# The last loads in another order, and one block of w2 loaded in mid-stream as 125 rows and 3 rows

## The chip, the core and the metric

The kernel runs on one core of one Trainium2 chip. The metric is the device time of one execution in microseconds (us), as the median of several runs. The engines of the core work side by side: TensorE (PE: matrix products, its weight loads are PEld), VectorE (DVE), ScalarE (ACT), GpSimd (POOL) and SyncE (SP), whose queue issues all the transfers of this kernel. The transfers themselves are carried by 16 DMA engines, from HBM (the large memory) into SBUF (the on-chip memory of 128 partitions). PSUM is where TensorE leaves its sums. Everything is 32-bit floating point.

## The reference, cut to what matters

One decode step of a transformer block with a modulated layer norm: one token, D = 640, 32 heads of 192, a cache of 8192 positions, a feed-forward width F = 1536.

```python
mod = (silu(c) @ w_mod).reshape(1, 6, 1, -1)        # w_mod: 640 x 3840
sa, ca, ga, sb, cb, gb = mod[:, 0], ..., mod[:, 5]
h = layernorm(x) * (1 + ca) + sa
# attention: q = h @ wq; scores against k_cache, softmax, sum over v_cache, then @ wo
x = x + ga * attention(h, k_cache, v_cache, wq, wo)
h = layernorm(x) * (1 + cb) + sb
r = relu(h @ w1 + b1)                               # w1: 640 x 1536
x = x + gb * ((r * r) @ w2 + b2)                    # w2: 1536 x 640
```

The keys and the values are 32 x 8192 x 192 numbers each, 403 MB together; with all weights the kernel reads 452 MB once.

## The kernel before, in words

**The stream.** The host packs everything into few arrays whose rows belong to the 128 partitions. `plan()` cuts keys, values and the blocks of wq and wo that belong to them into 53 chunks of at most 84 x 192 numbers per partition (`SLOT`); a chunk is a tuple (first key, keys, first value unit, value units, extra blocks). `load(n)` (line 210 issues) takes the next of three buffers (`slot`, three in rotation) and issues the transfer on SP's queue; the last chunk goes in two pieces. After the 53 chunks three more loads follow, each into the next of the same three buffers, and each cut in pieces at the columns of a tuple:

- `wm1_t`: the last pair's block of wo (1920 columns) and the modulation columns 2 to 4, in two pieces (`WM_CUT`): 3840 KB and 1920 KB;
- `w1_t`: the modulation column 5 (for gb, 3200 columns) and w1 (5 blocks of 1536 columns), in two pieces (`W1_CUT`): 3904 KB and 1536 KB;
- `w2_t`: w2 as 12 blocks of 640 columns, in three pieces (`W2_CUT`): 2560, 960 and 320 KB, the last of them a single block.

`load(n + 3)` stands at the end of the turn of chunk n, so a load is issued when the work on the chunk three before it, which used the same buffer, is done. So wm1 goes into the buffer of chunk 50, w1 into that of 51 and w2 into that of 52.

**A chunk's work.** DVE multiplies keys by the query (line 249; the query stands in the ring `qb`) and sums (257), with a part of the sum begun on POOL (376). `softmax` follows when a head is complete; `values` adds the value units on PE (298), `evict` and `turn` bring a head pair's result into columns, and `attend` (331, 333) multiplies it by the pair's block of wo into the PSUM tile `att_a`.

**The end, in program order.** After the last chunk: `evict`, `turn(15)` and `attend(15)` with the block of wo in `wm1_t`; `mod(2, 3, ...)` (line 179), five steps of four matmuls for modulation columns 2 to 4, with `gather()` before its fourth step, which brings `att_a` through `att_s` into the layout of the rest (340 to 346); x1 (414, 415); `layernorm` "ln2": two sums over the partitions by a matmul with ones (line 137), with DVE work before, between and after; `columns`, which is DVE's transpose into hT (122). Then `gate(5, gb_t)` (188, 192): ten matmuls for gb and four copies by ACT. Then `ps_f` (428), 20 matmuls with w1; bias, relu and square on DVE (431 to 433), transpose (122); one matmul `ps_warm` whose result nobody reads (438); `ps_y` (446), 48 matmuls with w2, block b = 0 to 11 in order; two DVE steps (449, 450) and the output transfer (451).

The order of the work on each engine is the program order (`manual_schedule`); waits between engines are set by what each instruction reads and writes.

Of the kernel before, what the change touches and what calls it, by code (L numbers as in the profile page):

```python
# [8 lines left out]
F32 = mybir.dt.float32  # L9
# [4 lines left out]
P = 128  # L14
D = 640
H = 32
SK = 8192
DH = 192
FF = 1536
G = 4  # L20
DG = D // G
FG = FF // G
KB = DG // 32
FB = FG // 32
# [4 lines left out]
NPAIR = H // 2  # L29
NPOS = SK // P  # L30
POOL = 7
WO = 3 * D
QC = 512
NQ = H * DH // QC
RING = 3 * QC
SRING = 4 * NPOS
WQ = KB * QC
UNIT = E * DH
SLOT = 84 * DH
VPC = 5  # L40
LEAD_FROM = 1300
LEAD = 120
W1_CUT = (KB * D + 3 * FF, KB * D + KB * FF)
W2_CUT = (8 * D, 11 * D, 12 * D)
WM_CUT = (WO + 9 * D, WO + 15 * D)
WARM = 1
EPS = 1e-5


def plan():  # L50

    chunks, kp, vp, q, o = [], 0, 0, 1, 0
    while kp < H * NPOS or vp < H * NPOS // E:
        room, w = SLOT, []
        if o < NPAIR - 1 and 2 * (o + 1) * NPOS // E <= vp:
            w.append(("o", o))
            o, room = o + 1, room - WO
        used = (QC * (q - 2) - 1) // DH + 1 if q > 2 else 0
        if q < NQ and kp >= NPOS * (QC * q // DH) - 3 * NPOS // 2 and kp >= NPOS * used:
            w.append(("q", q))  # L60
            q, room = q + 1, room - WQ
        if not chunks:
            nk, nv = NPOS, 0
        else:
            v = VPC - 1 if kp >= LEAD_FROM else VPC
            nk = min(H * NPOS - kp, (room - v * UNIT) // DH)
            if kp + nk - E * (vp + v) > LEAD:
                v += 1
                nk = min(H * NPOS - kp, (room - v * UNIT) // DH)
            nv = min(H * NPOS // E - vp, (room - nk * DH) // UNIT)  # L70
            while nv and ((vp + nv - 1) // (NPOS // E) + 1) * NPOS > kp + nk:
                nv -= 1
            nk = min(H * NPOS - kp, (room - nv * UNIT) // DH)
        chunks.append((kp, nk, vp, nv, w))
        kp, vp = kp + nk, vp + nv
    assert q == NQ and o == NPAIR - 1
    return chunks


def width(chunk):  # L80
    return chunk[1] * DH + chunk[3] * UNIT + sum(WO if t == "o" else WQ for t, _ in chunk[4])


PLAN = plan()


@with_exitstack
def block_kernel(ctx: ExitStack, tc: tile.TileContext, kv, wm0, wm1, w1, w2, out):
    nc = tc.nc
    const = ctx.enter_context(tc.tile_pool(name="const", bufs=1))  # L90
    strm = ctx.enter_context(tc.tile_pool(name="strm", bufs=3))
    work = ctx.enter_context(tc.tile_pool(name="work", bufs=2))
    psum = ctx.enter_context(tc.tile_pool(name="psum", bufs=1, space=bass.MemoryType.PSUM))
# [25 lines left out]
    def columns(src, n, name, pool=const, **how):  # L119

        t = pool.tile([P, n // 32, 32], F32, name=name, **how)
        nc.vector.transpose(t.rearrange("p b r -> p (b r)"), src)
        return t
# [9 lines left out]
    def total(src, name):  # L133

        n = src.shape[1]
        ps = psum.tile([P, 512], F32, tag="sm", name="ps_" + name, bufs=2)
        nc.tensor.matmul(ps[:, :n], ones, src, start=True, stop=True)
        return ps[:, :n]

    def layernorm(x, copies, scale1, shift, name):  # L140

        n = x.shape[1]
        s = const.tile([P, 1], F32, name=name + "_s")
        nc.vector.tensor_reduce(s, x, axis=AX.X, op=ALU.add)
        m = const.tile([P, 1], F32, name=name + "_m")
        tm = total(s, name + "_tm")
        nc.vector.tensor_scalar(m, tm, 1.0 / (copies * D), None, op0=ALU.mult)
        xm = const.tile([P, n], F32, name=name + "_xm")
        nc.vector.tensor_scalar(xm, x, m, None, op0=ALU.subtract)
        sq = const.tile([P, n], F32, name=name + "_sq")  # L150
        ss = const.tile([P, 1], F32, name=name + "_ss")
        nc.vector.scalar_tensor_tensor(sq, xm, 1.0, xm, op0=ALU.mult, op1=ALU.mult, accum_out=ss)
        sd = const.tile([P, 1], F32, name=name + "_sd")
        nc.scalar.activation(sd, total(ss, name + "_tv"), AF.Sqrt, bias=eps_t, scale=1.0 / (copies * D))
        rs = const.tile([P, 1], F32, name=name + "_rs")
        nc.vector.reciprocal(rs, sd)
        h = const.tile([P, n], F32, name=name + "_h")
        nc.vector.scalar_tensor_tensor(h, xm, rs, scale1(), op0=ALU.mult, op1=ALU.mult)
        nc.vector.tensor_add(h, h, shift())
        return h  # L160
# [19 lines left out]
                                 wb[:, :, DG * g:DG * (g + 1)], start=(b == 0), stop=(b == KB - 1))  # L180
        nc.vector.tensor_copy(mods[:, first:first + n], ps[:, :n * DG].rearrange("p (m n) -> p m n", m=n))

    def gate(m, w):

        ps = psum.tile([P, 512], F32, tag="q", name=f"ps_mod{m}", bufs=2)
        for b in range(KB):
            for k in range(2):
                nc.tensor.matmul(ps[64 * k:64 * (k + 1), :2 * DG], e[:, b:b + 1].to_broadcast([P, 64]),  # L188
                                 w[:, b, 2 * DG * k:2 * DG * (k + 1)], start=(b == 0), stop=(b == KB - 1))
        for g in range(G):  # L190
            r = slice(32 * g, 32 * (g + 1))
            nc.scalar.activation(mods[r, m], ps[r, DG * (g % 2):DG * (g % 2 + 1)], AF.Copy)

    chunk_t = {}
    start = [sum(width(c) for c in PLAN[:n]) * P for n in range(len(PLAN))]

    def load(n):
        if n < len(PLAN):
            chunk_t[n] = slot(f"chunk{n}")
            m = width(PLAN[n])  # L200
            cuts = (m,) if n + 1 < len(PLAN) else ((PLAN[n][3] + 1) // 2 * UNIT, m)
            pieces = [(kv[start[n]:start[n] + P * m].rearrange("(p n) -> p n", p=P), cuts)]
        else:
            name, src, cuts = (("wm1_t", wm1, WM_CUT), ("w1_t", w1, W1_CUT), ("w2_t", w2, W2_CUT))[n - len(PLAN)]
            chunk_t[name] = slot(name)
            n, pieces = name, [(src, cuts)]
        for src, cuts in pieces:
            a = 0
            for b in cuts:
                nc.sync.dma_start(chunk_t[n][:, a:b], src[:, a:b])  # L210
                a = b
# [9 lines left out]
        return ca1  # L221

    h1 = layernorm(x_c, 1, scale_a, lambda: ma[:, :KB, 0], "ln1")
    qb = const.tile([P, RING], F32, name="qb")

    def query(u, w):
        w = w.rearrange("p (b n) -> p b n", b=KB)
# [4 lines left out]


    att_a = psum.tile([P, 512], F32, tag="att", name="att_a")
    att_s = const.tile([P, D], F32, name="att_s")
    nc.vector.memset(att_s, 0.0)
    query(0, wm0_t[:, KB * 2 * D:KB * 2 * D + WQ])

    sc = const.tile([P, SRING], F32, name="sc")
# [97 lines left out]

    def gather():

        nc.vector.tensor_copy(att_s[96:, :512], att_a[96:, :512])  # L340
        for j in range(NV):
            r = slice(32 * j, 32 * (j + 1))
            nc.scalar.activation(att_s[r, 512:], att_a[r, (D - 512) * j:(D - 512) * (j + 1)], AF.Copy)
        att_t.append(psum.tile([P, 512], F32, tag="o", name="att", bufs=3))
        for g in range(G):
            nc.tensor.matmul(att_t[0][32 * g:32 * (g + 1), :DG], sel.to_broadcast([P, 32]),
                             att_s[:, DG * g:DG * (g + 1)], start=True, stop=True)
# [6 lines left out]
    for n, (kp, nk, vp, nv, extra) in enumerate(PLAN):  # L354
# [3 lines left out]
        at = nk * DH + nv * UNIT  # L358
        wo_t = None
        for what, k in extra:  # L360
            w = t[:, at:at + (WO if what == "o" else WQ)]
            at += w.shape[1]
            if what == "q":
                query(k, w)
            else:
                wo_t = (k, w)
# [29 lines left out]
        for v in range(vp, vp + nv):  # L396
            if v % (NPOS // E) == NPOS // E - 1:
                to_evict.append(v // (NPOS // E))
        if wo_t is not None:
            attend(*wo_t)  # L400
        load(n + 3)

    wm1_t, w1_t, w2_t = chunk_t["wm1_t"], chunk_t["w1_t"], chunk_t["w2_t"]
    gb_t = w1_t[:, :KB * D].rearrange("p (b n) -> p b n", b=KB)
    w1_t = w1_t[:, KB * D:KB * (FF + D)].rearrange("p (b n) -> p b n", b=KB)
    w2_t = w2_t[:, :FB * D].rearrange("p (b n) -> p b n", b=FB)

    for h in to_evict:
        evict(h)
    turn(NPAIR - 1)  # L410
    attend(NPAIR - 1, wm1_t[:, :WO])
    mod(2, 3, wm1_t[:, WO:WO + KB * 3 * D].rearrange("p (b n) -> p b n", b=KB), gather)
    x1 = const.tile([P, DG], F32, name="x1")
    nc.vector.tensor_mul(x1, att_t[0][:, :DG], mods[:, 2])
    nc.vector.tensor_add(x1, x1, x_t)
# [3 lines left out]
        nc.vector.tensor_scalar(cb1, mods[:, 4], 1.0, None, op0=ALU.add)  # L419
        return cb1  # L420

    hT2 = columns(layernorm(x1, 32, scale_b, lambda: mods[:, 3], "ln2"), DG, "hT2")

    gate(5, gb_t)
    pf = psum.tile([P, 512], F32, tag="q", name="ps_f", bufs=2)
    for b in range(KB):
        for g in range(G):
# [5 lines left out]
    nc.vector.tensor_mul(f, f, f)  # L433
    fT = columns(f, FG, "fT", work, tag="om", bufs=1)

    idle = psum.tile([P, 512], F32, tag="sm", name="ps_warm", bufs=2)
    for k in range(WARM):
        nc.tensor.matmul(idle, ones, w1_t[:, k, :512], start=True, stop=True)
    gb2 = const.tile([P, DG], F32, name="gb2")
    nc.vector.tensor_mul(gb2, mods[:, 5], bbt[:, FG:])  # L440
    nc.vector.tensor_add(x1, x1, gb2)
# [1 line left out]
    py = psum.tile([P, 512], F32, tag="q", name="ps_y", bufs=2)  # L443
    for b in range(FB):
        for g in range(G):
            nc.tensor.matmul(py[32 * g:32 * (g + 1), :DG], fT[:, b], w2_t[:, b, DG * g:DG * (g + 1)],
                             start=(b == 0), stop=(b == FB - 1))
    y = const.tile([P, DG], F32, name="y")
    nc.vector.tensor_mul(y, py[:, :DG], mods[:, 5])
# [44 lines left out]
```

## Time and profile before

| | |
|---|---|
| median of 3 runs | 1056.03 us (1055.54 to 1056.21) |
| the profiled execution, its own time | 1055.57 us |
| its span, first to last instruction | 1053.8 us |
| busy: DVE, PE, POOL, ACT | 79%, 47%, 18%, 4% |
| DMA over the span | 452.15 MB, mean 429 GB/s |
| mean granted TensorE clock | 0.713 |

How to read it: the page cuts the span into 40 slices and gives in tenths how busy each engine was; the row of DMA engines stands at 9 in every slice but the last, where it is 7. The chain of work that ended last goes back from the last instruction, at each step to what released it. A view of the stretches gives, for chosen windows, each engine's busy time with its number of instructions, the granted clock, the mean busy share of the 16 DMA engines and their rate. The list of DMA issues gives the size of a transfer and the time from its issue on SP's queue to its landing. An instruction on PE that is written in 32-bit floating point shows as two records.

### The profile page before, as it was taken

Reading aid. Unit: us, or ns where it says so; the run is one execution under the profiler, and the core shown is the slowest. Engines: PE = TensorE matmul, PEld = TensorE weight load, DVE = VectorE, ACT = ScalarE, POOL = GpSimd, SP = SyncE. Lnnn points to the kernel's source line nnn. Section 1 sums busy time; section 2 is a strip of 40 time slices with the busy share of each in tenths; the row PEclk is TensorE's granted clock in tenths of the full one; section 3 lists DMA queues with packets and bytes.
Section 4 is the critical chain, followed back from the end, with each engine's and each line's share of the span. In section 5 each row is a group of like instructions: output and inputs, shape, how many; then the busy total and the mean of one; then the engine's idle time right before and its main releaser. Section 6 shows DMA issues by size and latency. Waiting matters only on the chain.

```text
span 1053.8 us, 5121 instructions
## 1 busy us (share of the span) xinstructions
PE 495.8 (47%) x2102; PEld 134.6 (13%) x2102; DVE 830.2 (79%) x428; ACT 43.4 (4%) x122; POOL 188.1 (18%) x57
## 2 busy tenths in 40 slices
PE   2153335455352363536344357344446346345286
PEld 1010011011010010101011011011011011011023
DVE  2898878877959969887797895999887977988822
ACT  1000000000000000000000000000000000000001
POOL 0212121121212202212121121122211211211200
PEclk9676576777675686668676577676777767768699
DMA  9999999999999999999999999999999999999997
GB/s 408 434 429 431 429 441 438 441 431 433 430 431 431 432 433 430 433 435 438 435 427 436 433 427 430 436 439 433 431 432 431 432 436 433 437 433 430 419 431 311
DMA packets 8959, 452.15 MB, mean 429 GB/s; under 512 B 996, under 2 KB 1000, under 8 KB 1256
## 3 DMA queue, kind: packets, MB, share of 16 engines
q1 hardware_dynamic: 8936, 451.83, 99.3%
q8 instruction: 16, 0.26, 0.1%
q14 instruction: 7, 0.06, 0.0%
HBM read 451.82 MB, written 0.00 MB: 429 GB/s over the span
## 4 chain that ended last, share of the span: by engine, by line
DMA 56%; DVE 31%; PE 11%; ACT 1%; issue 0%; SPq 0%; DVEq 0%
DMA chunk<-in_kv 53%; DVE chunk L249 16%; DVE sc L257 13%; PE ps_o L298 5%; DMA w_t<-in_w 2%; PE ps_q L230 2%; PE att_a L331 2%; DMA wm_t<-in_wm 1%; DVE os L312 1%; DVE om L310 1%; ACT p L281 0%; PE ps_mod L179 0%; PE ps_mx L273 0%; PE ps_mod L188 0%; PE att_a L333 0%
## 5 line engine op out<-in xcount | busy, mean ns | idle before, releaser
L249 DVE TENSOR_TENSOR chunk<-chunk,qb 128x8064 f32<-128x8064 f32 (+19 forms) x81 | 419.7, 5211 | 128.4 <-DMA chunk<-in_kv 123.2
L257 DVE TENSOR_REDUCE sc<-chunk 128x25 f32<-128x4800 f32 (+21 forms) x109 | 333.9, 3097 | 0.4
L298 PE MATMUL ps_o<-chunk,p 128*32 128x512 f32 x1536 | 296.7, 736 | 73.7 <-DMA chunk<-in_kv 64.3
L376 POOL TENSOR_TENSOR chunk<-chunk 128x1824 f32<-128x1824 f32 (+9 forms) x51 | 187.4, 3674 | 806.3 <-DVE chunk L249 548.4
L273 PE MATMUL ps_mx<-ident,mp 128*128 128x128 f32 x32 | 14.6, 455 | 343.9 <-DVE mp L271 343.9
L298 PEld LDWEIGHTS ps_o<-chunk,p 128*32 128x32 f32 x1536 | 67.4, 131 | 278.1 <-issue 188.1
L331 PE MATMUL att_a<-chunk,oT 128*32 128x512 f32 x90 | 63.4, 863 | 42.2 <-DVE oT L321 42.2
L230 PE MATMUL ps_q<-chunk,ln_h 128*128 128x512 f32 x110 | 66.9, 769 | 26.1 <-DMA chunk<-in_kv 26.1
L273 PEld LDWEIGHTS ps_mx<-ident,mp 128*128 128x128 f32 x32 | 5.6, 176 | 373.0 <-DVE mp L271 304.0
L281 ACT ACTIVATE p<-sc,nm 128x256 f32<-128x256 f32 x32 | 16.2, 507 | 649.9 <-DVE nm L275 649.9
L230 PEld LDWEIGHTS ps_q<-chunk,ln_h 128*128 128x128 f32 x110 | 26.5, 252 | 64.5 <-issue 35.1
L310 DVE TENSOR_TENSOR om<-ps_o,mask 96x512 f32<-96x512 f32 x32 | 21.6, 675 | 8.5 <-PE ps_o L298 8.5
L275 DVE TENSOR_REDUCE nm<-ps_mx 128x1 f32<-128x128 f32 x32 | 9.3, 292 | 19.5 <-PE ps_mx L273 19.5
L312 DVE TENSOR_REDUCE os<-om 96x64 f32<-96x512 f32 x32 | 21.8, 682 | 1.1
L331 PEld LDWEIGHTS att_a<-chunk,oT 128*32 128x32 f32 x90 | 11.7, 145 | 77.4 <-DVE oT L321 44.4
L320 DVE TENSOR_REDUCE oT<-ps_oT 128x3 f32<-128x96 f32 x16 | 4.0, 248 | 20.3 <-PE ps_oT L316 20.3
L286 PE MATMUL ps_sum<-ident,wide 128*128 128x128 f32 x16 | 7.5, 467 | 22.4 <-ACT wide L284 22.4
L179 PE MATMUL ps_mod<-wm_t,silu 128*32 128x320 f32 (+1 forms) x80 | 9.2, 608 | 15.5 <-DVE silu L167 15.5
L316 PE MATMUL ps_oT<-ident,os 96*128 96x96 f32 x16 | 5.0, 313 | 22.3 <-DVE os L312 22.3
L333 PE MATMUL att_a<-chunk,oW 128*96 128x384 f32 x30 | 14.1, 550 | 0.0
L231 ACT ACTIVATE qb<-ps_q 128x512 f32<-128x512 f32 x12 | 7.2, 597 | 136.7 <-PE ps_q L230 136.7
L329 ACT ACTIVATE oW<-oT 128x96 f32<-128x96 f32 x16 | 4.5, 280 | 177.5 <-DVE oT L321 177.5
(84 smaller groups left out, 100.9 us busy)
## 6 DMA issues: line engine op xcount, KB each, us to landing
chunk<-in_kv SPq DMA_DIRECT2D x38, 8064.0 KB, 37.5
chunk<-in_kv SPq DMA_DIRECT2D x11, 8000.0 KB, 38.3
chunk<-in_kv SPq DMA_DIRECT2D x2, 7872.0 KB, 38.5
chunk<-in_kv SPq DMA_DIRECT2D x1, 6144.0 KB, 27.6
wm_t<-in_wm SPq DMA_DIRECT2D x1, 4493.5 KB, 13.6
w_t<-in_w SPq DMA_DIRECT2D x1, 3904.0 KB, 20.7
wm_t<-in_wm SPq DMA_DIRECT2D x1, 3840.0 KB, 23.8
chunk<-in_kv SPq DMA_DIRECT2D x1, 3072.0 KB, 28.2
```

The lines of the kernel that those rows point to most:

```text
L230: nc.tensor.matmul(ps, h1[:, b:b + 1].to_broadcast([P, P]), w[:, b], start=(b == 0), stop=(b == KB - 1))
L249: nc.vector.tensor_mul(pr, pr, q[:, None, :].to_broadcast([P, b - a, DH]))
L257: nc.vector.tensor_reduce(sc[:, a % SRING:a % SRING + b - a], src[:, a - first:b - first], axis=AX.X, op=ALU.add)
L273: nc.tensor.transpose(ps[:, :P], mp.to_broadcast([P, P]), ident)
L275: nc.vector.tensor_reduce(nm, ps[:, :P], axis=AX.X, op=ALU.max, negate=True)
L281: nc.scalar.activation(p, s[:, :, None].to_broadcast([P, NPOS, 32 // E]), AF.Exp, bias=nm, accum_out=sp[:, h % 2:h % 2 + 1])
L298: nc.tensor.matmul(ps_t[h][32 * g:32 * (g + 1)], p[:, E * j:E * (j + 1)].rearrange("p e r -> p (e r)"), t[:, g], start=(j == 0), stop=last)
L310: nc.vector.tensor_mul(om[:n], ps_t.pop(h)[:n].rearrange("p (d e) -> p d e", e=E), mask[:n, None, :].to_broadcast([n, ED, E]))
L312: nc.vector.tensor_reduce(os_[:n, h % 2], om[:n], axis=AX.X, op=ALU.add)
L331: nc.tensor.matmul(att_a[96:, :512], oT[:, j:j + 1].to_broadcast([P, 32]), w[:, j, :512], start=(first and j == 0), stop=(last and j == NV ...
L333: nc.tensor.matmul(att_a[:96, :NV * (D - 512)], oW.rearrange("p j r -> p (j r)"), w[:, :, 512:], start=first, stop=last)
L376: nc.gpsimd.tensor_add(half, half, kt[:, m:, DH // 2:])
```

## The change

The diff has three parts.

1. **The order of the end.** The last block of wo (1920 columns, for pair 15) leaves `wm1` and stands at the end of the last chunk; `attend(15)` reads it there, and in program order it now comes after the load of w2 into that chunk's buffer. The modulation column 5 leaves `w1` and stands at the front of `wm1`. The pieces become: last chunk 3072 and 3264 KB; wm1 4480 and 1920 KB; w1 2304 and 1536 KB; w2 (11 blocks, without block 0) 1600, 1280 and 640 KB, the last of them two blocks.
2. **Block 0 of w2** (640 columns of 128 rows, 320 KB) is read into a tile of its own, `w2x_t`, by two transfers issued on SP's queue: rows 0 to 124 after chunk 20's turn, rows 125 to 127 after chunk 21's. They read w2 where it lies, 2560 B of each row.
3. **The order of the instructions.** `gate` becomes a generator: its matmuls come in three portions (two, one and two of its five steps) inside `layernorm`: ahead of the first sum over the partitions, behind that sum, and behind the second sum with ACT's square root. The four copies follow after hT. The matmul `ps_warm` goes. `att_s` and `qb` share one buffer (to pay for `w2x_t`), and `att_s` is cleared by POOL in `gather` instead of by DVE near the start.

```diff
+EXTRA = {"o": WO, "q": WQ}
-W1_CUT = (KB * D + 3 * FF, KB * D + KB * FF)
-W2_CUT = (8 * D, 11 * D, 12 * D)
-WM_CUT = (WO + 9 * D, WO + 15 * D)
-WARM = 1
+W1_CUT = (3 * FF, KB * FF)
+FIVE = {20: (0, 125), 21: (125, P)}
+WM_CUT = (KB * D + 9 * D, KB * D + 15 * D)
...
     assert q == NQ and o == NPAIR - 1
+    chunks[-1][4].append(("o", NPAIR - 1))
...
-    def layernorm(x, copies, scale1, shift, name):
+    def layernorm(x, copies, scale1, shift, name, between=lambda: None):
...
         m = const.tile([P, 1], F32, name=name + "_m")
+        between()
         tm = total(s, name + "_tm")
+        between()
...
         nc.scalar.activation(sd, total(ss, name + "_tv"), AF.Sqrt, bias=eps_t, scale=1.0 / (copies * D))
+        between()
...
-    def gate(m, w):
+    def gate(m, w, steps):
 
         ps = psum.tile([P, 512], F32, tag="q", name=f"ps_mod{m}", bufs=2)
-        for b in range(KB):
-            for k in range(2):
-                nc.tensor.matmul(ps[64 * k:64 * (k + 1), :2 * DG], e[:, b:b + 1].to_broadcast([P, 64]),
-                                 w[:, b, 2 * DG * k:2 * DG * (k + 1)], start=(b == 0), stop=(b == KB - 1))
+        b = 0
+        for n in steps:
+            for b in range(b, b + n):
+                for k in range(2):
+                    nc.tensor.matmul(ps[64 * k:64 * (k + 1), :2 * DG], e[:, b:b + 1].to_broadcast([P, 64]),
+                                     w[:, b, 2 * DG * k:2 * DG * (k + 1)], start=(b == 0), stop=(b == KB - 1))
+            b += 1
+            yield
         for g in range(G):
             r = slice(32 * g, 32 * (g + 1))
             nc.scalar.activation(mods[r, m], ps[r, DG * (g % 2):DG * (g % 2 + 1)], AF.Copy)
+        yield
...
+    w2x_t = const.tile([P, D], F32, name="w2x_t")
...
-            name, src, cuts = (("wm1_t", wm1, WM_CUT), ("w1_t", w1, W1_CUT), ("w2_t", w2, W2_CUT))[n - len(PLAN)]
+            name, src, cuts = (("wm1_t", wm1, WM_CUT), ("w1_t", w1, W1_CUT), ("w2_t", w2[:, D:], (5 * D, 9 * D, 11 * D)))[n - len(PLAN)]
...
-    qb = const.tile([P, RING], F32, name="qb")
+    qb = work.tile([P, RING], F32, name="qb", tag="qb", bufs=1)
...
-    att_s = const.tile([P, D], F32, name="att_s")
-    nc.vector.memset(att_s, 0.0)
...
     def gather():
 
+        att_s = work.tile([P, D], F32, name="att_s", tag="qb", bufs=1)
+        nc.gpsimd.memset(att_s, 0.0)
...
-        if wo_t is not None:
+        if wo_t is not None and n + 1 < len(PLAN):
             attend(*wo_t)
         load(n + 3)
+        if n in FIVE:
+            a, b = FIVE[n]
+            nc.sync.dma_start(w2x_t[a:b], w2[a:b, :D])
...
-    attend(NPAIR - 1, wm1_t[:, :WO])
-    mod(2, 3, wm1_t[:, WO:WO + KB * 3 * D].rearrange("p (b n) -> p b n", b=KB), gather)
+    attend(*wo_t)
+    mod(2, 3, wm1_t[:, KB * D:KB * 4 * D].rearrange("p (b n) -> p b n", b=KB), gather)
...
-    hT2 = columns(layernorm(x1, 32, scale_b, lambda: mods[:, 3], "ln2"), DG, "hT2")
-
-    gate(5, gb_t)
+    last = gate(5, gb_t, (2, 1, 2))
+    hT2 = columns(layernorm(x1, 32, scale_b, lambda: mods[:, 3], "ln2", lambda: next(last)), DG, "hT2")
+    next(last)
+
...
-    idle = psum.tile([P, 512], F32, tag="sm", name="ps_warm", bufs=2)
-    for k in range(WARM):
-        nc.tensor.matmul(idle, ones, w1_t[:, k, :512], start=True, stop=True)
...
-            nc.tensor.matmul(py[32 * g:32 * (g + 1), :DG], fT[:, b], w2_t[:, b, DG * g:DG * (g + 1)],
+            nc.tensor.matmul(py[32 * g:32 * (g + 1), :DG], fT[:, b], (w2_t[:, b - 1] if b else w2x_t)[:, DG * g:DG * (g + 1)],
```

More of the change, by code (lines that the diff above doesn't have):

```diff
@@ L76, in plan @@
     assert q == NQ and o == NPAIR - 1
+    chunks[-1][4].append(("o", NPAIR - 1))
     return chunks
 def width(chunk):
-    return chunk[1] * DH + chunk[3] * UNIT + sum(WO if t == "o" else WQ for t, _ in chunk[4])
+    return chunk[1] * DH + chunk[3] * UNIT + sum(EXTRA[t] for t, _ in chunk[4])
 PLAN = plan()
@@ L360, in block_kernel @@
         for what, k in extra:
-            w = t[:, at:at + (WO if what == "o" else WQ)]
+            w = t[:, at:at + EXTRA[what]]
             at += w.shape[1]
@@ L398, in block_kernel @@
                 to_evict.append(v // (NPOS // E))
-        if wo_t is not None:
+        if wo_t is not None and n + 1 < len(PLAN):
             attend(*wo_t)
         load(n + 3)
+        if n in FIVE:
+            a, b = FIVE[n]
+            nc.sync.dma_start(w2x_t[a:b], w2[a:b, :D])
     wm1_t, w1_t, w2_t = chunk_t["wm1_t"], chunk_t["w1_t"], chunk_t["w2_t"]
-    gb_t = w1_t[:, :KB * D].rearrange("p (b n) -> p b n", b=KB)
-    w1_t = w1_t[:, KB * D:KB * (FF + D)].rearrange("p (b n) -> p b n", b=KB)
-    w2_t = w2_t[:, :FB * D].rearrange("p (b n) -> p b n", b=FB)
+    gb_t = wm1_t[:, :KB * D].rearrange("p (b n) -> p b n", b=KB)
+    w1_t = w1_t[:, :KB * FF].rearrange("p (b n) -> p b n", b=KB)
+    w2_t = w2_t[:, :(FB - 1) * D].rearrange("p (b n) -> p b n", b=FB - 1)
     for h in to_evict:
@@ L476 @@
     kv = [np.concatenate([k[:, kp:kp + nk].reshape(P, -1), v[:, vp:vp + nv].reshape(P, -1)]
-                         + [(wo if what == "o" else wq)[i] for what, i in extra], axis=1).reshape(-1)
+                         + [{"o": wo, "q": wq}[what][i] for what, i in extra], axis=1).reshape(-1)
           for kp, nk, vp, nv, extra in PLAN]
@@ L482 @@
                                column(B_b1, FB), column(B_b2, KB)], axis=1),
-        "wm1": np.concatenate([wo[-1], rows(wm[:, 2 * D:5 * D], KB)], axis=1),
-        "w1": np.concatenate([rows(wm[:, 5 * D:], KB), rows(B_w1, KB)], axis=1),
+        "wm1": np.concatenate([rows(wm[:, 5 * D:], KB), rows(wm[:, 2 * D:5 * D], KB)], axis=1),
+        "w1": rows(B_w1, KB),
         "w2": rows(B_w2, FB),
```

## The prediction

> **What bounds the kernel now.** I read the page first, then the end of the chain of waits, the issues of the last loads, and the last microseconds in stretches.
>
> ```profile
> span 1053.8 us, 5121 instructions
> ...
> q1 hardware_dynamic: 8936, 451.83, 99.3%
> ...
> DMA 56%; DVE 31%; PE 11%; ACT 1%; issue 0%; SPq 0%; DVEq 0%
> ```
>
> The loads hold the 16 DMA engines for 99.3% of the span: up to the end the kernel is bound by bytes, and the change moves bytes without adding any. So only the end can pay. The chain of waits there, and PE's records of ps_y:
>
> ```profile
> 1015.98 20.69 DMA w_t<-in_w
> ...
> 1036.71 4.43 PE ps_mod L188 x20
> 1041.14 3.41 PE ps_f L428 x40
> ...
> 1044.57 0.57 DVE f L431
> ...
> 1046.98 3.50 PE ps_y L446 x96
> ...
> 1050.51 0.34 DVE y L449
> ```
> ```profile
> L446 PE MATMUL ps_y<-w_t,fT x96: 296/299/323, 1047.0 to 1050.1; 128*32 128x160 f32 x96
> ```
>
> From the landing of w1's first piece (1036.7) on, the chain is computation: gate 4.43, ps_f 3.41, from ps_f's end to ps_y 2.43 (1044.55 to 1046.98), ps_y 3.50. That looks as if a shorter computation would shorten the kernel. The issues say how far:
>
> ```profile
> 998.97 0.81 SPq L210 DMA_DIRECT2D wm_t<-in_wm  x2
> ```
> ```profile
> 1015.98 0.80 SPq L210 DMA_DIRECT2D w_t<-in_w  x2
> ```
> ```profile
> 1022.14 1.28 SPq L210 DMA_DIRECT2D w_t<-in_w  x3
> ```
> ```profile
> w_t<-in_w SPq DMA_DIRECT2D x1, 3904.0 KB, 20.7
> wm_t<-in_wm SPq DMA_DIRECT2D x1, 3840.0 KB, 23.8
> ...
> w_t<-in_w SPq DMA_DIRECT2D x1, 2560.0 KB, 24.3
> ...
> wm_t<-in_wm SPq DMA_DIRECT2D x1, 1920.0 KB, 28.1
> w_t<-in_w SPq DMA_DIRECT2D x1, 1536.0 KB, 24.0
> w_t<-in_w SPq DMA_DIRECT2D x1, 960.0 KB, 26.3
> w_t<-in_w SPq DMA_DIRECT2D x1, 320.0 KB, 26.6
> ```
>
> Issue plus time to landing, the issues of one row some 0.4 apart: wm1 at 1022.8 and 1027.5, w1 at 1036.7 and 1040.4, w2 at 1046.4, 1048.9 and 1049.6. PE's last record of ps_y starts at 1050.1 and ends at about 1050.45. Records start 0.033 apart ((1050.1 - 1047.0)/95) and last 0.30, so the last block (8 records) begins at 1050.45 - 0.30 - 7 x 0.033 = 1049.9, only 0.3 after its bytes. The last landing is a second bound right under the chain.
>
> And the landing itself is late, because the 16 DMA engines don't end together:
>
> ```profile
> 1044.00:1045.00 1.00, 1.00 (x10) 0.30 (x2) 0.43 (x1) 0.00 (x0) 0.00 (x0) 1.00 0.91 376
> 1045.00:1046.00 1.00, 0.55 (x2) 0.00 (x0) 0.93 (x3) 0.00 (x0) 0.00 (x0) 1.00 0.72 294
> 1046.00:1047.00 1.00, 0.02 (x3) 0.05 (x5) 0.93 (x4) 0.00 (x0) 0.00 (x0) 1.00 0.58 241
> 1047.00:1048.00 1.00, 1.00 (x32) 1.00 (x36) 0.29 (x1) 0.00 (x0) 0.00 (x0) 1.00 0.48 197
> 1048.00:1049.00 1.00, 1.00 (x37) 1.00 (x32) 0.00 (x0) 0.00 (x0) 0.00 (x0) 1.00 0.34 119
> 1049.00:1050.00 1.00, 1.00 (x37) 1.00 (x32) 0.00 (x0) 0.00 (x0) 0.00 (x0) 1.00 0.01 3
> ```
>
> The last two figures are the DMA engines' mean share and GB/s. Half the engines are done by about 1046.5 to 1047, the others work on to 1049. The shares sum to 3.04, so evenly loaded engines would end at 1047.0 instead of about 1049.1: **2.1 us is all that balancing could bring**, 0.2% of the time and about what a measurement of this kernel can tell from no change.
>
> **The change part by part.**
>
> *The order of the end.* The bytes up to the end of w1's first piece are the same 15040 KB from the last chunk on (5376 + 5760 + 3904 before, 6336 + 6400 + 2304 after). The stream's price is 3840 KB of w2 in 1049.6 - 1040.4 = 9.2, or 2.40 us per 1000 KB. The last block of wo comes with the last chunk, 960 KB more, 2.3 later; PE reads the units in front of it until 1022, so nothing waits. wm1 grows by 640 KB behind those 960: its pieces land 1600 x 2.40/1000 = 3.8 later, at 1026.6 and 1031.3. The first is in time for mod; the second holds mod's last eight matmuls:
>
> ```profile
> 1030.81 1.79 PE L179 MATMUL ps_mod<-wm_t,silu 128*32 128x480 f32 x16
> 1036.71 2.93 PE L188 MATMUL ps_mod<-w_t,silu 128*64 128x320 f32 x10 [0.41 <-DMA w_t<-in_w]
> 1039.43 1.71 PE L188 MATMUL ps_mod<-w_t,silu 128*64 128x320 f32 x10
> 1044.43 1.12 PE L438 MATMUL ps_warm<-w_t,ones 128*128 128x512 f32 x2
> ```
> ```profile
> 1034.08 0.32 DVE L144 TENSOR_REDUCE ln_s<-x 128x1 f32<-128x160 f32 x1
> 1037.75 0.34 DVE L122 STREAM_TRANSPOSE hT<-ln_h 128x160 f32<-128x160 f32 x1
> ```
>
> They start at 1031.3 instead of 1030.8, so mod, the layer norm and hT slip 0.5: hT is ready at 1038.6 (1038.1 before). On SP the load of w2 may wait for attend(15) in chunk 52's buffer, until 1028.1 (1022.1 before); SP has only the output transfer behind it and the DMA engines have w1 until 1040.4, so I count nothing. Without that cover it would cost up to 6.
>
> *The gate.* Its 20 records take 0.17 each in the second half (1.71/10), 0.29 in the first. Eight go between mod's end (1033.1) and the first sum (1034.9): 1.4 into a gap of 1.8. Four go beside about 1.0 of DVE work before the second sum (0.7); eight go beside the 1.8 from that sum to hT (1.4). I count no delay; at 0.29 each the two eights would overrun by 0.5 each. So 4.43 leaves the chain. ps_f starts at hT, 1038.6, needs w1's second piece (1040.4) at its fourth step, 1038.6 + 3 x 0.68 = 1040.6, ends at 1042.0, and ps_y can start at 1044.5: **2.5 earlier**. ACT's four copies come behind the square root as before, and their reader stands on DVE behind fT. Without ps_warm 1.12 of PE's idle time there is no longer filled; it was never in the chain.
>
> *w2's bytes.* ps_y needs blocks 1 to 5 at about 1044.7. Without block 0 the pieces land at 1040.4 + 3.8 = 1044.2, + 3.1 = 1047.3, + 1.5 = 1048.8. So PE takes six blocks, waits, takes four, waits, and ends with two. **The late thing is now the last landing L**: two blocks end 0.04 + 15 x 0.033 + 0.30 = 0.84 after it, where before the end stood 0.85 after its own L. Of the 2.5 only the shift of L remains.
>
> *Where block 0's bytes go.* Spread over 16 engines the 320 KB cost each 0.77 in mid-stream and save 0.77 at the end: L stays, gain 0. On five engines (125 rows have no even split between 5 and 25, and the diff calls the table FIVE) each of the five carries 62.5 KB: at 16 x 2.40/1000 = 0.038 per KB, 2.4 us, and 0.1 more for one of the three rows; all 16 save 20 KB, 0.77. So eleven engines end 0.77 earlier and five 1.73 later. If the five are among those done by 1047, they end by about 1048.8, just as the others do (1049.6 - 0.8). The trace names no engine, so which five is the choice on which the forecast hangs. What makes an engine late can be guessed at from two rows:
>
> ```profile
> q8 instruction: 16, 0.26, 0.1%
> q14 instruction: 7, 0.06, 0.0%
> ```
>
> Apart from the one queue there are only instruction fetches: 16 of 16 KB, each about 1 us of its engine (0.1% of 16 x 1053.8, over 16). If every engine had served one, all would be equally late. Half are late by some 2 to 3, so an estimate from these rows is that the fetches fall on one half, twice each; then five engines that stand together in number are likelier all early or all late than mixed. I take five engines, and the early half at two to one against any late one among them; all the other ends are rivals. [...]
>
> *Edits at nothing.* The two issues in mid-stream:
>
> ```profile
> SPq L210 <- DVE sc L257: 752.5, 50, 24.9
> ```
> ```profile
> L236 DVE MEMSET att_s<- x1: 592/592/592, 24.1 to 24.1; 128x640 f32 x1
> ```
> ```profile
> 991.11 3.84 POOL L376 TENSOR_TENSOR chunk<-chunk 128x1728 f32<-128x1728 f32 x1 [14.08 <-DVE chunk L249]
> ```
>
> SP waits 15 us at a time for a buffer (752.5/50), so two issues of 0.4 hide there. DVE's memset goes from a stretch before the first chunk's work. POOL's last sum ends at 995; a memset, below that 3.84, is over 25 us ahead of gather (1028). Uncovered it would cost up to 3.8.
>
> **Sum.** L from 1049.6 to 1048.8; 0.1 given back since the five may end last. The profiled execution took 1055.57 (span 1053.8 and 1.8 around it), so 1054.9. The shown runs lie up to 0.6 above that execution and their median 0.46; I add 0.2: **1055.1 us**, its own range 1054.4 to 1056.0.
>
> **The rivals.**
>
> *The five include late engines* (slower than before). An engine that ended after 1047.9 has no room for 1.73. One of the latest lands at 1049.6 + 1.7 = 1051.3, the end comes 1.7 later: 1057.3, with two blocks at half clock 1057.9. For it: half of the engines are late and no row names them. Against it: only the guess about the fetches and an even chance between the halves, so I give it half the weight of the main case.
>
> *The transfer is spread anyway*: L unchanged, 1055.6 to 1056.
>
> *PE's clock falls while it waits.*
>
> ```profile
> 1033.00:1036.40 3.40, 0.71 (x4) 0.59 (x4) 2.09 (x8) 0.06 (x1) 0.00 (x0) 1.00 0.96 407
> 1036.40:1039.80 3.40, 3.09 (x12) 1.48 (x14) 1.36 (x5) 0.20 (x1) 0.00 (x0) 0.50 1.06 447
> ```
>
> After 3.4 us with 0.71 busy the granted clock was 0.50, and the gate's records took 0.29 instead of 0.17. After the change PE idles 2.5 before ps_y, then 1 more before the second piece. At half clock a block costs some 0.27 more: 0.5 if only the last two are hit, 1.5 if all are and they queue past L: 1055.6 to 1056.6. Where the stretches of the clock begin decides it; I hold a costly hit for the rarer case. [...]
>
> **Chances.** Main 0.47, spread 0.13, clock 0.13, late engines 0.24, something unforeseen 0.03. Faster by over 0.2% (below 1053.9) needs the whole 2.1: 0.04. Slower by over 0.2% (above 1058.1): half of the late case (the one with half clock and what lies above it) and the unforeseen, 0.15. The rest, 0.81, lies within. The range, 1054.2 to 1058.0, leaves out those ends.
>
> **What would show it.** The gate's 20 records before hT, ps_f at about 1038.6, ps_y at about 1044.5 with waits on in_w inside it, and its end 0.84 after the last landing. With the five among the early ones the DMA share stays over 0.7 to about 1047 and falls within two microseconds; with late ones it has a tail of 0.3 (5 of 16) to 1051. Wrong it would be if ps_y isn't held by w2, or if a chunk after 20 lands so late that DVE idles.

## The result, and the profile after

The changed kernel takes **1059.53 us** (median of 6 runs, 1059.41 to 1059.88) against 1056.12 us (median of 6, 1055.54 to 1056.65) for the kernel before: a ratio of 1.0032 with a 95% interval of 1.0021 to 1.0043. It is 3.4 us slower, where 1055.1 was forecast in a range of 1054.2 to 1058.0. Its profiled execution took 1059.53 with a span of 1057.8, 4.0 more than the span before.

The end of the chain of waits after (start, length, what), and PE's records of ps_y from the timeline:

```profile
1033.49 20.00 DMA w_t<-in_w
...
1053.54 0.80 PE ps_y L457 x16
...
1054.36 0.34 DVE y L460
```
```profile
1048.93 0.48 PE L457 MATMUL ps_y<-w2x_t,fT 128*32 128x160 f32 x8 [2.37 <-DVE fT L123]
1049.20 1.57 PE L457 MATMUL ps_y<-w_t,fT 128*32 128x160 f32 x40
1051.99 1.29 PE L457 MATMUL ps_y<-w_t,fT 128*32 128x160 f32 x32 [1.22 <-DMA w_t<-in_w]
1053.54 0.75 PE L457 MATMUL ps_y<-w_t,fT 128*32 128x160 f32 x16 [0.26 <-DMA w_t<-in_w]
```

The computation has left the chain: ps_y is cut up by waits for w2, and the last landing stands at 1053.5 with two blocks behind it. But that landing came at 1049.6 before. The stretches of the end show what it waited for (the last two columns are the share of the 16 DMA engines and GB/s):

```profile
1048.00:1049.00 1.00, 0.07 (x4) 0.10 (x8) 0.96 (x3) 0.00 (x0) 0.00 (x0) 1.00 0.79 328
1049.00:1050.00 1.00, 1.00 (x32) 1.00 (x36) 0.33 (x1) 0.00 (x0) 0.00 (x0) 1.00 0.55 206
1050.00:1051.00 1.00, 0.77 (x24) 0.45 (x15) 0.00 (x0) 0.00 (x0) 0.00 (x0) 1.00 0.06 26
1051.00:1052.00 1.00, 0.01 (x3) 0.02 (x3) 0.00 (x0) 0.00 (x0) 0.00 (x0) 1.00 0.06 26
1052.00:1053.00 1.00, 1.00 (x32) 0.92 (x32) 0.00 (x0) 0.00 (x0) 0.00 (x0) 1.00 0.06 26
```

For some 2.5 to 3 us a share of 0.06, one sixteenth, at 26 GB/s: **a single DMA engine works on alone**. In the records of the single packets the other fifteen are done at about 1050.3, and the lone one at 1053.04; a landing follows the last packet by some 0.4 (1053.04 to 1053.49 here, 1049.17 to 1049.6 before), so the fifteen would land at about 1050.7. And that is later than 1049.6 less the 0.8 that each of them was spared. The rest was lost in mid-stream. The stretch around the new transfer, before and after:

```profile
440.00:500.00 60.00, 31.11 (x116) 8.50 (x117) 47.81 (x27) 2.67 (x8) 9.90 (x3) 0.72 1.01 435
460.00:480.00 20.00, 10.80 (x50) 2.64 (x50) 17.47 (x11) 0.91 (x3) 4.99 (x2) 0.67 1.02 439
```
```profile
440.00:500.00 60.00, 27.89 (x99) 7.85 (x102) 46.15 (x24) 2.39 (x7) 9.89 (x3) 0.66 1.01 421
460.00:480.00 20.00, 10.17 (x50) 2.57 (x50) 16.49 (x11) 0.91 (x3) 4.01 (x2) 0.67 1.01 391
```

The DMA engines are busy all the time (1.01) but move less: (435 - 421)/435 x 60 = 1.9 us of the whole stream's time. The second rows place it: within 460 to 480 the rate is 391 where it was 439. In the records of the single packets it is the time in which the 125 rows move (464.9 to 471.3); a 64000 B packet beside them took up to 3.65 us where 2.4 is usual. These records show the number of engines too, since an engine's part of a transfer ends there with a packet of 4 B (the lone engine's eight packets of 5120 B at 1053.04). A transfer of 128 rows has 16 of them; from 460 to 480 the DMA view counts 21 packets under 512 B where before it counts 16, and from 480 to 492, where the 3 rows move, 19 where before it counts 16. So the 125 rows ran on five engines and the 3 rows on three. The number of an engine stands in no record.

So the last landing moved by 1.9 (slow stretch), less 0.8 (w2 is a block shorter at the end), and by the 2.8 from 1050.7 to 1053.5 for one engine: 3.9.

### The profile page after: what moved, and what is told of

It is laid out like the page before. It is cut to its first block, busy times and chain, and to the rows that moved or that the text cites. A ratio compares the mean times of both kernels' runs of the same rounds, so it can differ in the third digit from the quotient of the medians.

```text
span 1057.8 us, 5120 instructions
## 1 busy us (share of the span) xinstructions
PE 488.8 (46%) x2100; PEld 132.1 (12%) x2100; DVE 829.8 (78%) x427; ACT 43.5 (4%) x122; POOL 188.7 (18%) x58
## 4 chain that ended last, share of the span: by engine, by line
DMA 56%; DVE 30%; PE 12%; ACT 1%; issue 0%; SPq 0%; DVEq 0%
DMA chunk<-in_kv 53%; DVE chunk L257 16%; DVE sc L265 12%; PE ps_o L306 6%; PE ps_q L240 2%; PE att_a L339 2%; DMA w_t<-in_w 2%; DMA wm_t<-in_wm 1%; DVE os L320 1%; DVE om L318 1%; PE ps_mod L183 1%; PE att_a L341 0%; ACT p L289 0%; PE ps_mx L281 0%; DVE nm L283 0%
## 5 line engine op out<-in xcount | busy, mean ns | idle before, releaser
L306 PE MATMUL ps_o<-chunk,p 128*32 128x512 f32 x1536 | 292.2, 726 | 75.4 <-DMA chunk<-in_kv 66.0
L339 PE MATMUL att_a<-chunk,oT 128*32 128x512 f32 x96 | 66.6, 851 | 43.0 <-DVE oT L329 43.0
L289 ACT ACTIVATE p<-sc,nm 128x256 f32<-128x256 f32 x32 | 16.2, 507 | 652.9 <-DVE nm L283 652.9
```

Of the source, the lines that this page charges most:

```text
L289: nc.scalar.activation(p, s[:, :, None].to_broadcast([P, NPOS, 32 // E]), AF.Exp, bias=nm, accum_out=sp[:, h % 2:h % 2 + 1])
L306: nc.tensor.matmul(ps_t[h][32 * g:32 * (g + 1)], p[:, E * j:E * (j + 1)].rearrange("p e r -> p (e r)"), t[:, g], start=(j == 0), stop=last)
L339: nc.tensor.matmul(att_a[96:, :512], oT[:, j:j + 1].to_broadcast([P, 32]), w[:, j, :512], start=(first and j == 0), stop=(last and j == NV ...
```

## The experiments

Theory A, from these rows: one of the five engines was already late, and a transfer on these five engines slows the whole stream. The rival, theory B: the new order of the end costs by itself. For the slow stretch there were three candidates: the pitch of w2's rows, the small number of engines, and the partitions that the engines write. All edits are against the changed kernel unless it is said.

**Block 0 on all 16 engines.**

```diff
-FIVE = {20: (0, 125), 21: (125, P)}
+FIVE = {20: (0, P)}
```

> Undoes one part: block 0 of w2 comes in one transfer of 128 rows after chunk 20, all else as in the changed kernel. Theory A (one of the five engines was already late, and the transfer on five engines slows the whole stream while it runs, some 2 us): both go, no stretch of the stream falls below 400 GB/s in mid-stream, the last landing comes back from 1053.5 to about 1049.6, no DMA engine works on alone at the end, 1055.3 to 1056.0 us. Theory B (the new order of the end costs by itself, since w2 is issued at 1032.6 instead of 1022.1): stays at 1058 to 1059.5 us.

Measured: 1056.04 us (1055.69 to 1056.66), a ratio to the kernel before of 0.9998 (0.9988 to 1.0007). The stretch of the stream, the end of the chain, and the last stretches:

```profile
440.00:500.00 60.00, 31.53 (x113) 8.65 (x114) 47.03 (x27) 2.67 (x8) 9.89 (x3) 0.69 1.01 435
```
```profile
1030.21 20.00 DMA w_t<-in_w
...
1050.26 0.79 PE ps_y L457 x16
...
1051.08 0.34 DVE y L460
```
```profile
1048.00:1049.00 1.00, 0.30 (x9) 0.29 (x13) 0.00 (x0) 0.00 (x0) 0.00 (x0) 1.00 0.26 108
1049.00:1050.00 1.00, 0.99 (x32) 0.65 (x20) 0.00 (x0) 0.00 (x0) 0.00 (x0) 1.00 0.05 20
1050.00:1051.00 1.00, 0.74 (x16) 0.42 (x16) 0.00 (x0) 0.00 (x0) 0.00 (x0) 1.00 0.00 0
```

435 GB/s again, the last landing at 1050.2, and the whole loss gone. Theory B falls. It shows something else too: with everything else of the change in place (the gate's matmuls in the layer norm's gaps, ps_warm gone, the order of the loads) the kernel is as fast as before, within the interval. ps_y begins at 1045.8, 1.2 us earlier than the 1047.0 of before, and all of that turned into waits for w2.

**The 125 and 3 rows alone, on the old order of the end** (edit against the kernel before, with the shared buffer of qb and att_s):

```diff
-W2_CUT = (8 * D, 11 * D, 12 * D)
+W2_CUT = (7 * D, 10 * D, 11 * D)
+FIVE = {20: (0, 125), 21: (125, P)}
...
+        if n in FIVE:
+            a, b = FIVE[n]
+            nc.sync.dma_start(w2x_t[a:b], w2[a:b, :D])
```

> Does one part alone: the old order of the end and of the instructions, with block 0 of w2 in 125 rows and 3 rows in mid-stream (and the shared buffer of qb and att_s that pays for it). Theory A: the stretch below 300 GB/s and the lone engine at the end are there as in the changed kernel, last landing 1053.5, the last piece is one block, so 1059.0 to 1059.6 us. Theory B: as before, 1055.5 to 1056.5 us.

Measured: 1060.08 us (1059.23 to 1061.59), ratio 1.0038 (1.0023 to 1.0052).

```profile
440.00:500.00 60.00, 28.02 (x96) 7.81 (x99) 46.67 (x24) 2.39 (x7) 9.96 (x4) 0.66 1.01 421
```
```profile
1051.26 3.50 PE ps_y L451 x96
```

The transfer by itself brings the whole loss, with the same 421 GB/s. The time lies 0.5 above that of the changed kernel and 0.5 above the upper end that I had given. In the profiled execution it is the longer computation of the old order that ends last: ps_y runs without a wait for w2 and ends at 1054.8, where it ended at 1054.3 in the changed kernel. There, for once, the shorter computation shows a little, though the ranges of the runs overlap.

**The same rows from a dense array.**

```diff
-            nc.sync.dma_start(w2x_t[a:b], w2[a:b, :D])
+            nc.sync.dma_start(w2x_t[a:b], w2x[a:b])
...
+        "w2x": np.ascontiguousarray(rows(B_w2, FB)[:, :D]),
```

> Changes one thing: the 125 rows and the 3 rows are read from an array of their own in which they lie one after another, not from w2's rows 30720 B apart. If the pitch of the rows in HBM makes the slow stretch, it goes, and the time falls by the 2 us that it costs, to about 1057.5 us (the lone late engine stays, 2.7 us behind the next). If the five engines or the partitions they write make it, nothing changes: 1059.3 to 1059.8 us, with the same fall below 300 GB/s.

Measured: 1059.61 us (1059.29 to 1059.73), ratio 1.0029 (1.0017 to 1.0041).

```profile
440.00:500.00 60.00, 28.14 (x99) 7.87 (x102) 46.05 (x24) 2.39 (x7) 9.88 (x3) 0.66 1.00 419
```

Nothing changes, so the pitch of w2's rows isn't the cause.

**Two transfers of 64 rows.**

```diff
-FIVE = {20: (0, 125), 21: (125, P)}
+FIVE = {20: (0, 64), 21: (64, P)}
```

> [...] If the slow stretch comes from engines writing each other's partitions, two stretches under 400 GB/s show and some 0.5 to 1.5 us stay: 1056.2 to 1057.2 us. If it comes from using few engines, none shows and the time is that of the transfer on 16 engines, 1055.3 to 1056.0 us.

Measured: 1058.66 us (1057.96 to 1059.39), ratio 1.0022 (1.0013 to 1.0031).

```profile
440.00:500.00 60.00, 28.06 (x102) 7.88 (x105) 46.83 (x24) 2.39 (x7) 10.11 (x4) 0.69 1.01 415
460.00:480.00 20.00, 9.71 (x50) 2.49 (x50) 16.38 (x11) 0.91 (x3) 3.89 (x2) 0.72 1.00 403
```

Here no engine ends alone (a share of 0.51 at 1050, 0.23 at 1051 and 0.00 at 1052), and the stream still loses (435 - 415)/435 x 60 = 2.8 us, more than with five engines, and more than the 0.5 to 1.5 that I had allowed. That 64 rows run on all 16 engines, four on each, is an estimate from the even splits seen above (128 rows on 16, 125 on five, 3 on three); no run shows it. If it holds, few engines aren't needed for the slow stretch. What this run shares with the 125 rows, and the run with 128 rows doesn't, is that the block comes in two transfers of fewer than 128 rows.

**The two halves one right behind the other**, so that all partitions get the same within the stretch:

```diff
-FIVE = {20: (0, 125), 21: (125, P)}
+FIVE = {20: (0, 64)}
...
             nc.sync.dma_start(w2x_t[a:b], w2[a:b, :D])
+            nc.sync.dma_start(w2x_t[b:], w2[b:, :D])
```

> The two transfers of 64 rows one right behind the other after chunk 20, so that over the stretch all 128 partitions get the same bytes and all 16 engines carry the same. If the two separate halves were slow because half of the partitions got all the bytes, the slow stretch shrinks and 1.0 to 1.6 us of the 2.4 us lost there come back: 1056.6 to 1057.5 us. If they were slow because engines write partitions that other engines are writing in their own loads, the loss stays: 1058.0 to 1059.2 us.

Measured: 1058.00 us (1057.27 to 1058.89), ratio 1.0017 (1.0007 to 1.0026).

```profile
440.00:500.00 60.00, 27.36 (x105) 7.81 (x108) 46.81 (x24) 2.39 (x7) 10.11 (x4) 0.72 1.00 418
```

2.3 us lost by this row instead of 2.8, and the time lies at the lower end of what I expected for a loss that stays. So an uneven load on the partitions can be a smaller part at most; the rest stays. Of what was tried, what is left is how the rows of a cut transfer are dealt out to engines and partitions. Which engine serves which row or partition stands in no run, and of the reading side only the pitch was tried. So the cause of the slow stretch was not shown; that the engines get in each other's way at the partitions stays a guess.

**124 rows, and 123.** By the same even split 124 rows would run on four engines, 31 on each, and 123 on three, 41 on each: an estimate, no run shows these two numbers.

```diff
-FIVE = {20: (0, 125), 21: (125, P)}
+FIVE = {20: (0, 124), 21: (124, P)}
```

> The split 124 and 4 instead of 125 and 3: 124 rows divide evenly by four, so four engines carry 31 rows (77.5 KB, 3.0 us) and one row more each. Theory A says that one of the five engines of the changed kernel was already late and ended alone. If that engine is the fifth, the lone engine goes, all end near 1051 and the time is 1057.0 to 1057.8 us (the slow stretch of some 2 us stays). If it is one of the first four, it carries 0.6 us more than before, ends alone near 1054, and the time is 1059.8 to 1060.5 us.

```diff
-FIVE = {20: (0, 125), 21: (125, P)}
+FIVE = {20: (0, 123), 21: (123, P)}
```

> The split 123 and 5: 123 rows divide by three, so three engines carry 41 rows each (102.5 KB, 3.9 us). If the late engine is the fourth or the fifth, it carries none of this but a row of the second transfer, and the three early ones end near 1051.3: 1057.2 to 1058.0 us. If it is among the first three: an end alone near 1055, 1060.8 to 1061.5 us. The slow stretch is there in both cases.

Measured: with 124 rows 1060.53 us (1060.31 to 1060.76), ratio 1.0039 (1.0025 to 1.0052); with 123 rows 1059.00 us (1058.59 to 1059.66), ratio 1.0023 (1.0014 to 1.0033). The stretch of the stream and the end, first with 124 rows, then with 123:

```profile
440.00:500.00 60.00, 26.39 (x99) 7.41 (x102) 46.11 (x24) 2.39 (x7) 9.90 (x3) 0.69 1.01 419
...
1052.00:1053.00 1.00, 0.35 (x11) 0.04 (x6) 0.00 (x0) 0.00 (x0) 0.00 (x0) 0.50 0.06 26
1053.00:1054.00 1.00, 1.00 (x16) 0.75 (x20) 0.00 (x0) 0.00 (x0) 0.00 (x0) 0.50 0.06 26
```
```profile
440.00:500.00 60.00, 26.09 (x87) 7.31 (x90) 46.99 (x24) 2.39 (x7) 10.29 (x4) 0.69 1.00 413
...
1050.00:1051.00 1.00, 0.21 (x8) 0.00 (x0) 0.00 (x0) 0.00 (x0) 0.00 (x0) 1.00 0.44 179
1051.00:1052.00 1.00, 0.75 (x24) 0.73 (x28) 0.00 (x0) 0.00 (x0) 0.00 (x0) 1.00 0.20 82
1052.00:1053.00 1.00, 0.73 (x24) 0.40 (x20) 0.00 (x0) 0.00 (x0) 0.00 (x0) 1.00 0.03 10
```

With 124 rows the lone engine is there and works on past 1053, later than with 125; with 123 no engine works alone for long (a share of 0.03 at 1052, where the others had 0.06). So, if the estimate holds, the late engine belongs to a set of four and to one of five, not to one of three. Its number is not shown. These two runs were on one chip; the lone engine with five showed on another one too (the run with the dense array), but that it is the same engine there is not shown. The time with 123 rows missed what I expected by 1.0 us. Its stretch loses (435 - 413)/435 x 60 = 3.0 us, not the 2 that I had taken over from the five; with 124 rows (419) it is 2.2, with 125 (421) 1.9.

The rate in a window depends a little on where the window cuts the packets. All packets can be counted instead: by how much later than in the kernel before had the same number of bytes moved, behind the slow stretch, less the same ahead of it? Each figure is from one profiled execution.

| block 0 of w2 as | stream later by, us |
|---|---|
| one transfer of 128 rows | 0.1 |
| 125 and 3 rows; on the old order; from a dense array | 2.0; 2.0; 2.0 |
| 124 and 4 rows | 2.2 |
| 123 and 5 rows | 2.8 |
| two halves, apart | 2.7 |
| two halves, together | 2.0 |

So all the cut transfers cost the stream 2 to 3 us, and the whole one next to nothing beyond its bytes.

**One block in the last piece**, with block 0 on all 16 engines, and then **the same with two idle matmuls** between ps_f and ps_y:

```diff
-FIVE = {20: (0, 125), 21: (125, P)}
+FIVE = {20: (0, P)}
-            ("w2_t", w2[:, D:], (5 * D, 9 * D, 11 * D))
+            ("w2_t", w2[:, D:], (6 * D, 10 * D, 11 * D))
```

> The order of the end with block 0 in one transfer of 128 rows, and w2's pieces cut 6, 4 and 1 blocks instead of 5, 4 and 2. If the last landing is the bound, one block behind it instead of two saves 0.27 us: 1055.3 to 1056.0 us, 0.2 to 0.4 us under the run with two blocks. If something else bounds the end, no change.

```diff
+    idle = psum.tile([P, 512], F32, tag="sm", name="ps_warm", bufs=2)
+    for k in range(2):
+        nc.tensor.matmul(idle, ones, w1_t[:, k, :512], start=True, stop=True)
```

> The run with block 0 on all 16 engines and one block in the last piece, and two idle matmuls between ps_f and ps_y (some 1.7 us of PE in a gap of 2.4). In the run without them ps_y took 5.3 us at half clock and ended 0.9 after the last landing instead of 0.57. If PE's clock is what ate the saving, ps_y ends 0.57 after the last landing and the time is 1055.3 to 1055.9 us, 0.2 to 0.6 under the kernel before. If the last landing alone decides, no difference to the run without them: 1056.0 us.

Measured: 1056.10 us (1055.55 to 1056.72), ratio 0.9997 (0.9988 to 1.0006), and 1055.76 us (1055.69 to 1055.97), ratio 0.9995 (0.9986 to 1.0004). The stretch in which ps_y begins and the one in which it ends (the column before the last two is the granted clock), first without the idle matmuls, then with them:

```profile
1045.00:1048.00 3.00, 2.31 (x36) 1.49 (x40) 1.08 (x3) 0.00 (x0) 0.00 (x0) 0.65 0.62 256
1048.00:1051.00 3.00, 2.94 (x68) 2.02 (x60) 0.00 (x0) 0.00 (x0) 0.00 (x0) 0.78 0.13 48
```
```profile
1045.00:1048.00 3.00, 2.55 (x57) 1.65 (x56) 1.12 (x4) 0.00 (x0) 0.00 (x0) 1.00 0.63 257
1048.00:1051.00 3.00, 1.56 (x40) 1.20 (x40) 0.14 (x1) 0.00 (x0) 0.00 (x0) 1.00 0.12 48
```

The end of the chain with them:

```profile
1030.36 18.82 DMA w_t<-in_w
...
1049.23 1.61 PE ps_y L460 x40
```

Without them the saving of 0.27 isn't seen; the clock was down in the profiled execution. With them the clock stays at 1.00 there and the eleven runs lie within 0.3 us, where those without spread over 1.2. The time lies where I expected it, but not for the reason that I gave: ps_y ends at 1050.84, 0.9 after the last landing (1049.9) and not 0.57. The chain runs through the middle piece, which lands at 1049.18 with five blocks behind it, so a single block in the last piece cannot show its 0.27 here. The median is the lowest of the study, but the kernel before was lower beside it too (1056.12, against 1056.40 beside the run without them), and its interval to the kernel before holds 1: no version was found that is measurably faster than the kernel before.

## Why the prediction was wrong, and where it was right

**Which step failed.** It was "Where block 0's bytes go", in two places. First, I priced the transfer on five engines at 2.5 us for these five and at nothing for the other eleven. It cost the whole stream 1.9 us, since the other packets grew while it ran, and it cost the five more than 2.5: a row's packet took 0.165 us (median), where each of the 3 rows that follow at 488 took 0.11 and the rows of w2's last block in the kernel before 0.10; the packets of the 125 rows add up to 19.8 us, so 25 rows hold an engine for some 4. No rival had that, and no row of the trace before could show it: every transfer there, but the output's, has 128 rows. I should have kept a price from both sides for it; its own 2.5 us on all engines, as an upper end, on top of the late rival's 1057.3 reaches 1059.8 and would have held the result. Second, I took the five to be early engines. Four of them ended with the rest, one was late, and one is enough; that the five would be all early or all late rested on the guess that they are neighbours. No run shows which five they are, and the guess on their end failed. The rival "the five include late engines" named this with 1.7; measured, the last landing moved by 3.9, which is 2.0 without the slow stretch. The sign that I gave for it was a tail of 0.3, five engines; it was 0.06, one engine, and to 1053 instead of 1051.

Added up: the rival's 1057.3, and 1.9 for the slow stretch, is 1059.2; measured 1059.5.

**The order of the end** was right in what bounds it, and wrong in one time. The last landing became the bound, and ps_y ended 0.84 after it, as worked out (1053.49 to 1054.33). "Of the 2.5 only the shift of L remains" is the run with block 0 on all engines: nothing gained, 1056.04, at the upper edge of the 1055.6 to 1056 of the rival in which the transfer is spread. But the 2.5 itself didn't come in that run, since mod's last matmuls slipped by more than the 0.5 forecast:

```profile
1024.05 4.46 PE L339 MATMUL att_a<-chunk,oT 128*32 128x512 f32 x6 [0.69 <-DVE oT L329]
...
1032.60 1.82 PE L183 MATMUL ps_mod<-wm_t,silu 128*32 128x480 f32 x16 [0.45 <-DMA wm_t<-in_wm]
1034.34 1.30 PE L194 MATMUL ps_mod<-wm_t,silu 128*64 128x320 f32 x8
1036.64 0.76 PE L194 MATMUL ps_mod<-wm_t,silu 128*64 128x320 f32 x4
1038.04 1.30 PE L194 MATMUL ps_mod<-wm_t,silu 128*64 128x320 f32 x8
1040.00 3.43 PE L442 MATMUL ps_f<-w_t,hT 128*32 128x384 f32 x40 [0.67 <-PE ps_mod L194]
```

They start at 1032.60, 1.8 after the 1030.81 of before. The six records of attend(15) took 4.46 instead of 2.76, at a granted clock of 0.50 from 1026 to 1028 (1.00 before), and behind them came a wait of 0.45 for wm1's second piece, which landed at 1032.5 and not at 1031.3. So ps_y began 1.2 earlier instead of 2.5. From these matmuls on, the way to ps_y is 3.0 shorter than before (13.2 against 16.2). In the changed kernel, where attend(15) took 2.76, it is 2.5 shorter (1035.25 to 1048.93).

**The gate** fits into the gaps: 1.30, 0.76 and 1.30 against 1.4, 0.7 and 1.4, and ps_f starts behind hT. **SP's load of w2** was issued at 1032.6 in the changed kernel, behind attend(15), and cost nothing, as said: its first piece landed 16.2 later and the DMA engines were busy until then (a share of 0.79 at 1048).

**The clock** was a rival that decided nothing in the changed kernel's profiled execution (1.00 in all stretches of the end), since its two blocks fell into a stretch at full clock. But it is real: 0.50 in the last stretches of the run with 124 rows, 0.65 and 0.78 in the one with one last block, and 0.50 in attend(15) of the run with block 0 on all engines. The prediction looked for it only in ps_y.

**Balancing** could bring 2.1 at most, I wrote, and so nothing that can be told from no change. That bound held; it speaks of the gain alone, and the loss had no such bound.

## What to carry to other kernels

When the DMA engines are the bound, keep every transfer in the shape of the stream's own: a small one that came in fewer rows (312 KB in 125 rows, 320 KB in two halves) cost the whole stream 1.9 to 2.8 us, more than twice its share of 0.8. Before bytes are put on some engines to use their slack, each of these engines must be known to have it, since one late engine sets the end (1053.5, where the other fifteen would have landed at about 1050.7). When the computation in front of the last wait gets shorter, look first at the landing right behind it: here ps_y began 1.2 us earlier, with block 0 on all engines, and the time stayed.

## What the runs showed of the hardware that was not expected

- A transfer can slow others without any DMA engine standing idle: the share stays at 1.01 while the rate falls from 435 to 421 GB/s over 60 us (391 over the 20 around it). The share of busy time says nothing of it, only the rate does.
- Halving a transfer of 128 rows into two of 64 costs this stream some 2 us (together) to 2.8 us (apart), where the whole one costs nothing that can be seen (435 GB/s).
- The DMA engines don't end together: before, half of them still worked at 1047 (a share of 0.48), and of the five that took the extra rows one ended alone by 2.5 to 3 us. What makes it late wasn't tried; the guess on instruction fetches of the prediction stays a guess.
